# Unit 0's attention output turned on PE, zero matmuls tied to results, and new orders, in a fused window-attention and channel-mix kernel

## Chip, cores and metric

One core of a Trainium2 chip runs the whole program. The metric is the device time of one launch in microseconds (us).

## The reference, cut to what matters

Attention with a causal window of 128 keys and 4 sink keys, followed by a channel mix (a shift by one token, two mixes, and a gated two-layer product). The matmul operands are held in bf16 in the kernel.

```python
# q, k, v: 4 batches, 8 heads, 768 tokens, 64 wide; attention
scores = scale * q @ k.T                       # keep: key < 4, or 0 <= query - key < 128
a = exp(scores - max); a = a / sum(a)
x = (a @ v), heads side by side                # 4 x 768 x 512
# channel mix
x_prev = x shifted by one token
xk = mu_k * x + (1 - mu_k) * x_prev            # and xr with mu_r
k = relu(xk @ w_k)                             # 512 x 1024
out = sigmoid(xr @ w_r) * ((k * k) @ w_v)      # 512 x 512, 1024 x 512
```

## The kernel before

**Units.** The work is cut into 12 units of 256 tokens (u = 0 to 11, three for each batch, T = 0 to 2 within it), each unit into four pairs of heads. A unit goes through four stages: `prepare` (cast q, k, v to bf16; turn q and k by PE transposes or DMA transposes into `qt` and `kt`), `attend`, `mix`, and `ffn`, which follows one unit later.

**Attention.** For a pair, PE writes scores with keys on the partitions and queries in the columns into one of two wide PSUM tiles `sc`. ACT takes the exponential into `e`, DVE multiplies it by the window's mask (L901). PE then multiplies with `e` stationary and the values streaming (L920): the output has queries on the partitions and, per head, 64 columns and one more, the sum of the exponentials, since `vb` carries a column of ones. DVE takes the reciprocal of the four sums (L934, `rec`) and multiplies (L937) into `x`. In units with T > 0 the sink keys come in by a matmul of their own (L858, L873).

**Mix and channel mix.** The mix wants features on the partitions, so `x` is transposed: by PE into a bank (L961) and copied from there by ACT or DVE into `xt` (L970), or, for the units in `XD`, by DMA. DVE subtracts the shifted tile (L997, `td`) and makes `xk` and `xr` (L1010), one step for each 128 features. PE multiplies with `wk_sb` (L1087), ACT takes the relu (L1097, `rl`), DVE squares it (L1109, `kk`), PE multiplies with `wv_h` (L1136), and with `wr_sb` for the gate (L1118), ACT takes the tanh (L1124, `th`), DVE combines (L1145, `ob`), and SP or POOL stores.

**What sets the order.** Every step is an operation of a plan, with a number. The table `ORDER` gives each engine its list of numbers; `CHOICE` gives some steps their engine (ACT, DVE or POOL). `Plan.schedule` walks these lists with costs written into the kernel, and hands out the buffers: four PSUM banks (`bank`), two wide PSUM tiles (`sc`), five tiles `e` and so on. On the chip an engine works its list in order, and a step that waits holds up all behind it. Where the plan sees PE idle before 26 us of its own time, it puts in zero matmuls ("fills", L1160): a tile of zeros times a tile of zeros into a free bank. They wait for no data.

Of the kernel before, what the change touches and what calls it, by code (L numbers as in the profile page):

```python
# [18 lines left out]
    80: "ACT", 81: "POOL", 82: "ACT", 83: "POOL", 84: "POOL", 85: "ACT", 86: "ACT",  # L19
    88: "ACT", 90: "DVE", 96: "POOL", 98: "DVE", 99: "DVE", 101: "DVE", 102: "ACT",  # L20
    103: "ACT", 129: "POOL", 132: "DVE", 135: "POOL", 141: "ACT", 144: "DVE", 151:
    "DVE", 160: "PE/full", 172: "PE/full", 183: "POOL", 186: "DVE", 189: "POOL",
    192: "POOL", 195: "ACT", 196: "DVE", 198: "DVE", 242: "PE/full", 265: "DVE",
    268: "DVE", 271: "POOL", 273: "DVE", 274: "POOL", 277: "DVE", 278: "ACT", 352:
    "POOL", 355: "POOL", 361: "DVE", 380: "DVE", 428: "POOL", 432: "POOL", 438:
    "ACT", 496: "PE/full", 511: "POOL", 516: "ACT", 517: "ACT", 587: "POOL", 591:
    "ACT", 592: "ACT", 628: "POOL", 661: "POOL", 663: "POOL", 665: "ACT", 666:
    "ACT", 675: "DVE", 736: "POOL", 741: "ACT", 785: "POOL", 810: "POOL", 815:
    "DVE", 855: "POOL", 888: "DVE", 889: "ACT", 929: "POOL", 945: "PE/full", 998:
    "DVE", 1002: "DVE", 1006: "DVE", 1010: "DVE", 1019: "POOL",  # L30
# [7 lines left out]
BIAS = ()  # L38

# [55 lines left out]
    ),  # L95
    "DVE": (
# [25 lines left out]
    ),  # L122
    "ACT": (
# [14 lines left out]
    ),  # L138
    "POOL": (
# [3 lines left out]
    ),  # L143
# [8 lines left out]
    ),  # L152
}


class Plan:

    SEM = 40.0
    LAG = {"PE": 163.0, "DVE": 83.0, "ACT": 114.0, "POOL": 60.0, "SP": 90.0}

    def __init__(self):
        self.ops, self.pools, self.buf = [], {}, {}
        self.fill, self.fill_until = None, 0.0  # L170

# [15 lines left out]
    def schedule(self):  # L187
# [43 lines left out]
        while any(lines.values()):  # L231
# [35 lines left out]
            if o["port"]:  # L267
                port[o["engine"]] = t + (0.58 * cost if o["engine"] == "POOL" else cost)
# [953 lines left out]
```

## Time and profile before

| | |
|---|---|
| median of the runs shown | 166.06 us (165.44 the lowest) |
| the profiled execution | 166.53 us |
| its span (first to last instruction) | 164.4 us |
| mean granted clock of TensorE | 0.99 |
| busy: PE, DVE, ACT, POOL | 93%, 91%, 74%, 19% of the span |
| fills: L1165 x8 and L1162 x5, all before 28 us | 5.55 and 1.90 us of PE |

One of the three runs took 530.24 us; the median is the middle of the three. Busy time is the share of the span in which an engine worked on an instruction. PE is the matmul part of TensorE, PEld its weight loads; a chain of waits follows the last instruction back, at each step to what released it.

### The profile page before, as it was taken

The page shows a single profiled execution, that of the slowest core. Times are in us where ns is not written, and L with a number is a line of the kernel's source. Part 1 is how long each engine was busy: PE and PEld are TensorE (multiplying, and loading weights), DVE is VectorE, ACT ScalarE, POOL GpSimd, SP SyncE. Part 2 cuts the span into 40 slices and gives each one's busy share as a digit, 9 for nine tenths or more (in the row PEclk, how much of TensorE's full clock was granted, in tenths as well). Part 3 has the DMA queues.
Part 4 walks back from the last instruction along what each step waited for, and adds up shares of the span by engine and source line. Part 5 has one row for each costly group of instructions (what it writes and reads, how often), then busy time and mean ns, then how long its engine had stood idle before and what let it go on. Part 6 is the DMA issues. An engine that isn't in the chain of part 4 may idle for free.

```text
span 164.4 us, 4647 instructions
## 1 busy us (share of the span) xinstructions
PE 152.6 (93%) x1819; PEld 101.1 (61%) x1838; DVE 149.5 (91%) x383; ACT 121.7 (74%) x198; POOL 31.7 (19%) x61
## 2 busy tenths in 40 slices
PE   7988678899989999999999999999999999999991
PEld 2445557675448658677666766855485756578450
DVE  2599999999999999999999999998899989999931
ACT  3789989999989999999997689782499695152020
POOL 6633341312422023220201001032000100101001
PEclk9999789999999999999999999999999999999999
DMA  5999998999899999889988998999999933251032
GB/s 145 249 357 278 394 333 215 366 394 322 193 271 272 260 219 221 160 176 162 270 216 207 233 232 215 220 219 128 235 165 191 268 94 96 54 205 64 0 144 112
DMA packets 78821, 35.16 MB, mean 214 GB/s; under 512 B 68744, under 2 KB 71056, under 8 KB 78800
## 3 DMA queue, kind: packets, MB, share of 16 engines
q1 hardware_dynamic: 78384, 33.56, 84.0%
q0 software_dynamic: 400, 1.31, 2.3%
q8 instruction: 14, 0.23, 0.6%
q14 instruction: 7, 0.06, 0.1%
q10 hardware_dynamic: 16, 0.00, 0.0%
HBM read 24.12 MB, written 6.29 MB: 185 GB/s over the span
## 4 chain that ended last, share of the span: by engine, by line
PE 62%; DVE 24%; DMA 4%; POOL 4%; issue 3%; ACT 1%; DVEq 0%; POOLq 0%
PE bank L1087 21%; PE bank L1136 18%; PE bank L1118 8%; PE bank L920 6%; DVE e L901 5%; DMA kt<-kb 4%; PE sc L815 4%; DVE xr L1010 3%; DVE xk L1010 3%; DVE x L937 3%; DVE kk L1109 2%; DVE td L997 2%; PE bank L873 1%; POOL hmask L543 1%; PE bank L1057 1%
## 5 line engine op out<-in xcount | busy, mean ns | idle before, releaser
L1087 PE MATMUL bank<-xk,wk_sb 128*128 128x256 bf16 x384 | 47.6, 273 | 1.1 <-ACT rl L1097 0.5
L887 ACT ACTIVATE e<-sc 128x1024 bf16<-128x1024 f32 (+1 forms) x48 | 44.5, 967 | 2.8 <-PE sc L815 2.5
L1136 PE MATMUL bank<-wv_h,kk 128*128 128x512 bf16 x171 | 43.8, 379 | 0.8 <-DVE xk L1010 0.2
L1087 PEld LDWEIGHTS <-wk_sb 128*128 128x128 bf16 x384 | 36.2, 98 | 7.7 <-issue 1.5
L1097 ACT ACTIVATE rl<-bank 128x512 bf16<-128x512 f32 x43 | 25.2, 607 | 8.3 <-PE bank L1087 7.8
L901 DVE TENSOR_TENSOR e<-e,mask 128x1024 bf16<-128x1024 bf16 (+1 forms) x48 | 30.8, 656 | 0.0
L1124 ACT ACTIVATE th<-bank 128x512 f32<-128x512 f32 x24 | 14.3, 612 | 18.2 <-PE bank L1118 11.4
L1136 PEld LDWEIGHTS <-kk 128*128 128x128 bf16 x184 | 17.0, 98 | 16.5 <-issue 0.2
L1010 DVE SCALAR_TENSOR_TENSOR xr<-td,mu_all,xt 128x256 bf16<-128x256 bf16 x48 | 23.8, 507 | 0.0
L1118 PE MATMUL bank<-wr_sb,xr 128*128 128x512 bf16 x90 | 23.3, 379 | 0.3
L1010 DVE SCALAR_TENSOR_TENSOR xk<-td,mu_all,xt 128x256 bf16<-128x256 bf16 x48 | 23.3, 511 | 0.0
L1109 DVE TENSOR_TENSOR kk<-rl 128x512 bf16<-128x512 bf16 x48 | 19.8, 425 | 0.4 <-ACT rl L1097 0.2
L937 DVE TENSOR_TENSOR x<-bank,rec 128x256 bf16<-128x256 f32 x48 | 19.5, 418 | 0.4
L920 PE MATMUL bank<-vb,e 128*128 128x65 bf16 x352 | 16.8, 196 | 1.4 <-DVE e L901 1.1
L1145 DVE SCALAR_TENSOR_TENSOR ob<-th,bank 128x512 f32<-128x512 f32 x23 | 15.6, 681 | 1.9 <-PE bank L1136 1.1
L920 PEld LDWEIGHTS <-e 128*128 128x128 bf16 x352 | 14.2, 99 | 4.5 <-DVE e L901 1.9
L1118 PEld LDWEIGHTS <-xr 128*128 128x128 bf16 x96 | 9.0, 98 | 9.6
L815 PE MATMUL sc<-qt,kt 64*64 64x128 bf16 (+3 forms) x496 | 12.5, 226 | 0.1
L1152 POOL DMA_DIRECT2D out_dram<-ob x5 | 2.8, 570 | 46.8 <-DVE ob L1145 46.8
L815 PEld LDWEIGHTS <-kt 64*64 64x64 bf16 (+1 forms) x496 | 9.0, 106 | 3.3 <-issue 1.0
L997 DVE TENSOR_TENSOR td<-xt 128x512 bf16<-128x512 bf16 x24 | 10.1, 432 | 0.1
L663 POOL CAST kb<-ks 128x512 bf16<-128x512 f32 x6 | 5.3, 884 | 20.4 <-DMA ks<-in_k_dram 17.8
(87 smaller groups left out, 157.2 us busy)
## 6 DMA issues: line engine op xcount, KB each, us to landing
vs<-in_v_dram SPq DMA_DIRECT2D x24, 256.0 KB, 5.3
out_dram<-ob SPq DMA_DIRECT2D x18, 256.0 KB, 3.3
ks<-in_k_dram SPq DMA_DIRECT2D x16, 256.0 KB, 4.2
qs<-in_q_dram SPq DMA_DIRECT2D x12, 256.0 KB, 4.9
qs<-in_q_dram SPq DMA_DIRECT2D x6, 512.0 KB, 7.1
ks<-in_k_dram SPq DMA_DIRECT2D x4, 512.0 KB, 9.3
w<-in_moe_w_k_dram SPq DMA_DIRECT2D x2, 1024.0 KB, 8.6
w<-in_moe_w_v_dram SPq DMA_DIRECT2D x2, 1024.0 KB, 10.6
```

The lines of the kernel that those rows point to most:

```text
L815: nc.tensor.matmul(out=sc[keys, a, o0 + f0 - q0:o0 + f1 - q0], lhsT=lhs[rows, keys], rhs=qs[rows, f0:f1], start=u not in BIAS, stop=True, ...
L887: nc.scalar.activation(out=buf[ek][:, :, lo:], in_=buf[sck][:, :, lo:], func=AF.Exp, scale=scale)
L901: nc.vector.tensor_tensor(out=at, in0=at, in1=m, op=ALU.mult)
L920: nc.tensor.matmul(out=o[:, g, a, :], lhsT=e[:, a, e0:e0 + 128], rhs=rhs, start=(T == 0 and i == 0), stop=(i == len(blocks) - 1), skip_gro ...
L937: P.op("DVE", dve(256), lambda ok=ok, rk=rk, c=c: nc.vector.tensor_tensor(out=buf["x", u][:, :, 128 * c:128 * c + 128].rearrange("p g (a d ...
L1010: nc.vector.scalar_tensor_tensor(out=buf[key][:, c, :], in0=buf[tk][:, i, :], scalar=mu[w][:, c:c + 1], in1=xt[:, c, t0 - 1:t0 + 255], op0 ...
L1087: nc.tensor.matmul(out=ps[:, i, :], lhsT=wk_sb[:, c, 128 * f:128 * f + 128], rhs=xk[:, c, :], start=(c == 0), stop=(c == NC - 1), skip_gro ...
L1097: nc.scalar.activation(out=buf[rk], in_=buf[psk].rearrange("p (i t) -> p i t", i=2), func=AF.Relu)
L1109: P.op("DVE", dve(512, 0.52), lambda f2=f2, rk=rk: nc.vector.tensor_tensor(out=buf["kk", u][:, 2 * f2:2 * f2 + 2, :], in0=buf[rk], in1=buf ...
L1118: nc.tensor.matmul(out=buf[psk], lhsT=buf["xr", u][:, c, 128 * g:128 * g + 128], rhs=wr_sb[:, c, :], start=(c == 0), stop=(c == NC - 1))
L1136: nc.tensor.matmul(out=buf[psk], rhs=wv_h[:, f, :], lhsT=buf["kk", u][:, f, 128 * g:128 * g + 128], start=(f == 0), stop=(f == NF - 1))
L1145: P.op("DVE", dve(512), lambda psk=psk, tk=tk, bk=bk: nc.vector.scalar_tensor_tensor(out=buf[bk], in0=buf[tk], scalar=1.0, in1=buf[psk], o ...
```

## The change

1. **Unit 0 turned** (`TF = (0,)`). For unit 0, PE multiplies with the values stationary and the exponentials streaming. The output has the 64 features of a head on half of the partitions and 256 queries in the columns, so it needs no transpose. The sums come from the same exponentials against a tile of ones, into the other half of the bank: 64 equal rows for each head. DVE takes the reciprocal of all 128x256 sums into `den`, a new pool of two tiles, and multiplies straight into `xt`. For unit 0 the transposes on PE, their copies into `xt` and the products into `x` are gone.
2. **Tied zero matmuls.** After 4.6 us of the plan's time, and up to 28.5, a fill may stream a piece of a tile that DVE or ACT has just made (against the zero weights), and so waits for that result. It may also write into an `sc` tile.
3. **Costs and orders.** Some of the plan's costs are changed, and all of `ORDER` and `CHOICE` is written anew. Over the whole program ACT has 5 instructions fewer, DVE 4, POOL has 7 casts and 8 stores more, and SP 8 stores fewer.

The diff, cut to its core:

```diff
 CHOICE = {
-    80: "ACT", 81: "POOL", 82: "ACT", 83: "POOL", 84: "POOL", 85: "ACT", 86: "ACT",
+    80: "ACT", 81: "POOL", 82: "ACT", 83: "POOL", 84: "POOL", 85: "ACT", 87: "ACT",
...
+TF = (0,)
...
 ORDER = {
     "PE": (
-        91, 94, 107, 100, 97, 78, 118, 110, 115, 105, 130, 136, 143, 133, 139, 126,
+        91, 94, 78, 107, 100, 97, 118, 110, 115, 130, 121, 105, 136, 133, 139, 155,
...
+    PAUSE = 130.0
...
-            if o["engine"] == "PE" and self.fill:
+            if o["engine"] == "PE" and self.fill and before < 4600.0:
...
+            elif o["engine"] == "PE" and self.fill and before < self.fill_until:
+
+                last = max((j for j in o["after"]), key=lambda j: ops[j]["end"], default=None)
+                now, seen = before, before - 500.0
+                while now + 230.0 < t:
...
+                    gates = [j for j, e in done.items() if seen < e + self.SEM <= now and (
+                        last is not None and ops[j]["engine"] == ops[last]["engine"] or
+                        e < t - 700.0)]
+                    gate = max(gates, key=lambda j: done[j], default=None)
...
+                    order.append(("fill", tile_ if name == "bank" else tile_[:, 0, :], 1, gate))
...
+    pool("den", 2, [128, 256], FP32)
...
-                if T > 0:
+                if T > 0 and u not in TF:
...
+            def turned(c=c, ek=ek, ok=ok):
+                e, o = buf[ek], buf[ok]
+                for which in range(2):
+                    c0 = 256 * which
+                    for i in range(4 if T > 0 else 2):
+                        for a in range(2):
+                            h = 2 * c + a
+                            rows = slice(64 * a, 64 * a + 64)
+                            if i == 0:
+                                w, m, q0 = buf["vb", u][:, 0, h, 0:D], e[:, a, 128:384], 0
+                            elif i == 1:
+                                w, m, q0 = buf["vb", u][:, 1, h, 0:D], e[:, a, 384:512], 128
...
+                            if which:
+                                w = ones[:, 0:D] if i < 3 else hmask[:, h, 0:D]
+                            n = m.shape[-1]
+                            nc.tensor.matmul(out=o[rows, c0 + q0:c0 + q0 + n], lhsT=w, rhs=m,
+                                             start=(i == 0), stop=(i == (3 if T > 0 else 1)),
+                                             skip_group_check=True)
+
+            if u in TF:
...
+                P.op("DVE", dve(256), lambda ok=ok, dk=dk: nc.vector.reciprocal(
+                    out=buf[dk], in_=buf[ok][:, 256:512]), r + 1, hold=[ok], reads=[ok],
+                    take=[("den", dk)], writes=[dk])
+                P.op("DVE", dve(256), lambda ok=ok, dk=dk, c=c, xt=xt, t0=t0: nc.vector.tensor_tensor(
+                    out=xt[:, c, t0:t0 + 256], in0=buf[ok][:, 0:256], in1=buf[dk],
+                    op=ALU.mult), r + 1, hold=[ok, dk],
...
+                continue
...
-            if u not in XD:
+            if u in TF:
+                pass
+            elif u not in XD:
...
-    def fill(bank, wide):
-        if wide == 1:
+    def fill(bank, wide, gate=None):
+        if gate is not None:
+            nc.tensor.matmul(out=bank, lhsT=warm[:, 0:128], start=True, stop=True,
+                             rhs=part(gate)().unsqueeze(1).to_broadcast([128, 4, 128]))
+        elif wide == 1:
...
-    P.fill_until = 26000.0
+    P.fill_until = 28500.0
```

**DVE, unit 0's attention to unit 1's first mask.** A number after a name is the tile's. Before, from one of unit 0's last two masks to the first mask of unit 1 (e_97, 1024 columns):

```order
L901 TENSOR_TENSOR e_96<-e_96,mask_147 128x2x384
L970 COPY xt_155<-bank_66 128x2x256
L901 TENSOR_TENSOR e_95<-e_95,mask_147 128x2x384
L659 CAST qb_84<-qs_72 128x2x4x64
L997 TENSOR_TENSOR td_110<-xt_155 128x512
L934 RECIPROCAL rec_103<-bank_66 128x4
L934 RECIPROCAL rec_104<-bank_63 128x4
L937 TENSOR_TENSOR x_107<-bank_66,rec_103 128x2x128
L1010 SCALAR_TENSOR_TENSOR xk_113<-td_110,mu_all,xt_155 128x256
L1010 SCALAR_TENSOR_TENSOR xr_117<-td_110,mu_all,xt_155 128x256
L937 TENSOR_TENSOR x_107<-bank_63,rec_104 128x2x128
L901 TENSOR_TENSOR e_97<-e_97,mask 128x1024
```

And now, up to the same mask (a first wide reciprocal and its product stand just ahead of this piece):

```order
L970 RECIPROCAL den_111<-bank_65 128x256
L973 TENSOR_TENSOR xt_157<-bank_65,den_111 128x256
L970 RECIPROCAL den_110<-bank_64 128x256
L1073 TENSOR_TENSOR td_112<-xt_157 128x512
L934 TENSOR_TENSOR e_96<-e_96,mask_149 128x2x384
L1086 SCALAR_TENSOR_TENSOR xk_115<-td_112,mu_all,xt_157 128x256
L973 TENSOR_TENSOR xt_157<-bank_64,den_110 128x256
L1086 SCALAR_TENSOR_TENSOR xk_115<-td_112,mu_all,xt_157 128x256
L1086 SCALAR_TENSOR_TENSOR xr_119<-td_112,mu_all,xt_157 128x256
L800 TENSOR_TENSOR vsink_155<-bank_66,hmask 128x8x64
L970 RECIPROCAL den_111<-bank_63 128x256
L934 TENSOR_TENSOR e_97<-e_97,mask 128x1024
```

The casts of q and the copy into xt are gone from this piece; four reciprocals of 4 columns have become four of 256, all ahead of e_97's mask.

**PE, ahead of unit 1's first scores** (the matmuls into sc from qt_90 and kt_86). Before:

```order
L920 MATMUL bank_66<-vb_135,e_95 128x65
L1162 LDWEIGHTS warm
L1162 MATMUL bank_65<-warm 128x512
L815 LDWEIGHTS kt_86
L815 MATMUL sc_61<-qt_90,kt_86 64x192
```

Now:

```order
L736 MATMUL bank_63<-ident,qb_83 128x128
L1272 LDWEIGHTS warm
L1272 MATMUL sc_62<-td_112,warm 128x512
L1272 LDWEIGHTS warm
L1272 MATMUL sc_62<-e_96,warm 128x512
L848 LDWEIGHTS kt_86
L848 MATMUL sc_62<-qt_90,kt_86 64x192
```

The fill of zeros alone has become two that read td_112 and e_96, into the tile that the scores write next.

**POOL, in the middle of the program.** Before:

```order
L659 CAST qb_83<-qs_71 128x2x4x64
L757 COPY ksink_152<-kt_88 64x4x4 x2
L659 CAST kb_80<-ks_68 128x2x4x64
L663 CAST kb_81<-ks_69 128x4x128
L740 CAST vb_135<-vs_74 128x8x64
L663 CAST kb_81<-ks_69 128x4x128
```

Now:

```order
L692 CAST qb_83<-qs_71 128x2x4x64
L1228 DMA out_dram<-ob_135 128x512
L692 CAST qb_84<-qs_72 128x2x4x64
L696 CAST kb_81<-ks_69 128x4x128 x2
L773 CAST vb_137<-vs_74 128x8x64
L1228 DMA out_dram<-ob_136 128x512
L773 CAST vb_137<-vs_74 128x8x64
```

Stores of `ob` now stand between the casts for later units.

More of the change, by code (lines that the diff above doesn't have):

```diff
@@ L18 @@
 CHOICE = {
-    80: "ACT", 81: "POOL", 82: "ACT", 83: "POOL", 84: "POOL", 85: "ACT", 86: "ACT",
[L20 to L30, printed above, removed]
+    80: "ACT", 81: "POOL", 82: "ACT", 83: "POOL", 84: "POOL", 85: "ACT", 87: "ACT",
+    88: "ACT", 93: "DVE", 96: "POOL", 98: "DVE", 102: "DVE", 103: "DVE", 129:
+    "POOL", 132: "POOL", 141: "ACT", 179: "POOL", 182: "POOL", 185: "POOL", 188:
+    "POOL", 191: "DVE", 194: "DVE", 201: "DVE", 213: "DVE", 230: "POOL", 250:
+    "PE/full", 264: "POOL", 267: "POOL", 270: "POOL", 274: "DVE", 286: "DVE", 315:
+    "POOL", 348: "POOL", 350: "DVE", 351: "POOL", 397: "POOL", 401: "PE/full", 424:
+    "POOL", 428: "POOL", 430: "POOL", 433: "ACT", 434: "DVE", 509: "POOL", 512:
+    "ACT", 554: "POOL", 581: "POOL", 582: "POOL", 583: "POOL", 585: "POOL", 588:
+    "ACT", 624: "POOL", 659: "POOL", 661: "ACT", 662: "ACT", 700: "POOL", 735:
+    "POOL", 738: "ACT", 781: "POOL", 806: "DVE", 810: "ACT", 811: "ACT", 830: "DVE",
+    847: "POOL", 851: "POOL", 880: "DVE", 885: "ACT", 925: "POOL", 941: "PE/full",
+    970: "DVE", 974: "DVE", 987: "POOL", 991: "POOL", 994: "DVE", 1002: "DVE", 1015:
+    "POOL",
 }
@@ L226, in schedule @@
         slow, gone, fetch = 0.0, 0.0, list(FETCH)
+        done = {}
         released = {key: 0.0 for key in owner}
@@ L254, in schedule @@
             lines[o["engine"]].pop(0)
+            own = []
             for name, key in o["take"]:
@@ L267, in schedule @@
             if o["port"]:
-                port[o["engine"]] = t + (0.58 * cost if o["engine"] == "POOL" else cost)
+                port[o["engine"]] = t + (max(0.58 * cost, cost - 200.0) if o["engine"] == "POOL" else cost)
             end = t + cost + o["lag"]
@@ L297, in schedule @@
             o["start"], o["end"] = t, end
-            if o["engine"] == "PE" and self.fill:
+            if o["engine"] == "PE" and self.fill and before < 4600.0:
                 now = before
-                while t - now > (300.0 if now > 4000.0 else 600.0) and now < self.fill_until:
+                while t - now > (300.0 if now > 4000.0 else 600.0):
                     some = [b for b in free["bank"] if b[0] <= now]
@@ L311, in schedule @@
                     order.append(("fill", self.pools["bank"][b[1]], wide))
+            elif o["engine"] == "PE" and self.fill and before < self.fill_until:
+                last = max((j for j in o["after"]), key=lambda j: ops[j]["end"], default=None)
+                now, seen = before, before - 500.0
+                while now + 230.0 < t:
+                    some = [(b[0], name, b[1], b) for name in ("bank", "sc") for b in free[name]
+                            if b[0] <= now] + [b for b in own if b[1] in ("bank", "sc") and b[0] <= now]
+                    if not some:
+                        now += 60.0
+                        continue
+                    _, name, at_, b = min(some, key=lambda b: b[:3])
+                    tile_ = self.pools[name][at_]
+                    gates = [j for j, e in done.items() if seen < e + self.SEM <= now and (
[3 more added lines that the diff above has]
+                    if gate is not None:
+                        seen = done[gate] + self.SEM
+                    order.append(("fill", tile_ if name == "bank" else tile_[:, 0, :], 1, gate))
+                    now += 225.0
+                    if b is not None:
+                        free[name].remove(b)
+                        free[name].append((now, at_))
+                    now += self.PAUSE if gate is not None else 0.0
+            if o["engine"] in ("DVE", "ACT") and self.gate(i):
+                done[i] = end
             order.append(i)
@@ L630, in cast @@
                    "ACT": (act(1024), emit("ACT"), False)} |
-             ({} if half else {"POOL": (1100.0, emit("POOL"), True)}),
+             ({} if half else {"POOL": (1050.0, emit("POOL"), True)}),
              reads=[(name + "32", i)], writes=writes)
@@ L676, in prepare @@
                            "DVE": (341.0, cast(nc.vector.tensor_copy), True),
-                           "POOL": (620.0, cast(nc.gpsimd.tensor_copy), True)},
+                           "POOL": (600.0, cast(nc.gpsimd.tensor_copy), True)},
                      take=[] if half else [(name + "b", rk)],
@@ L740, in cast @@
                 return lambda: copy(out=buf["vb", u][:, g, :, 0:D], in_=buf["v", u][:, g, :, :])
-            P.op("POOL", 620.0, cast(nc.gpsimd.tensor_copy), rank,
-                 alts={"POOL": (620.0, cast(nc.gpsimd.tensor_copy), True),
+            P.op("POOL", 600.0, cast(nc.gpsimd.tensor_copy), rank,
+                 alts={"POOL": (600.0, cast(nc.gpsimd.tensor_copy), True),
                        "ACT": (515.0, cast(nc.scalar.copy), False),
@@ new lines, in attend @@
+            if u in TF:
+                P.op("PE", 700.0 if T else 360.0, turned, r + 1, mode=5, take=[("bank", ok)],
+                     hold=[ek, ("vb", u)] + ([("vb", u - 1), esk] if T else []), writes=[ok],
+                     reads=[ek, ("vb", u, 0), ("vb", u, 1), "ones0"] +
+                     ([esk, ("vsink", b % 2), "hmask", ("vb", u - 1, 1)] if T else []))
+                xt, t0 = xts[b % 2], 16 + 256 * T
+                dk = ("den", u, k)
+                P.op("DVE", dve(256), lambda ok=ok, dk=dk: nc.vector.reciprocal(
[4 more added lines that the diff above has]
+                    op=ALU.mult), r + 1, hold=[ok, dk],
+                    reads=[ok, dk, "edges"] + ([("xh", u, k - 1)] if k % 2 else []),
+                    writes=[("xt", b % 2, T, k // 2, g) for g in range(2)] if k % 2
+                    else [("xh", u, k)])
+                continue
@@ L975, in mix @@
                      alts={"ACT": (act(512), evacuate(nc.scalar.copy), False),
-                           "DVE": (dve(512, 0.52), evacuate(nc.vector.tensor_copy), True)},
+                           "DVE": (dve(512, 0.52), evacuate(nc.vector.tensor_copy), False)},
                      hold=[psk], reads=[psk],
@@ L1155, in ffn, with part @@
                  alts={"SP": (400.0, store(nc.sync), False),
-                       "POOL": (1100.0, store(nc.gpsimd), True)})
+                       "POOL": (600.0, store(nc.gpsimd), False)})
     zeros = warm.bitcast(FP32)
-    def fill(bank, wide):
-        if wide == 1:
+    def part(i):
+        o = P.ops[i]
+        key = o["writes"][0] if o["writes"] else ()
+        if not isinstance(key, tuple) or len(key) < 2:
+            return None
+        name, u = key[0], key[1]
+        if name == "wk":
+            return lambda: wk_sb[:, 0, 256 * u:256 * u + 128]
+        if name == "wr":
+            return lambda: wr_sb[:, 2 * u, 0:128]
+        if name == "wv":
+            return lambda: wv_h[:, 2 * u, 0:128]
+        if name == "e" and o["engine"] == "DVE":
+            return lambda: buf[key][:, 0, 384:512]
+        if name in ("kb", "qb") and not by_dma(name[0], u):
+            if octet(name[0], u):
+                return lambda: eights(buf[key[:2]])[:, 4 * key[2]].rearrange("p h d -> p (h d)")
+            return lambda: buf[key[:2]][:, 0, 4 * key[2]:4 * key[2] + 2, :].rearrange(
+                "p h d -> p (h d)")
+        if name == "x":
+            return lambda: buf["x", u][:, 0, 128 * key[2]:128 * key[2] + 128]
+        if name == "xt":
+            t0 = 16 + 256 * key[2]
+            return lambda: xts[u][:, 2 * key[3], t0:t0 + 128]
+        if name == "td":
+            return lambda: buf[key][:, 0, 0:128]
+        if name in ("xk", "xr") and len(key) == 3:
+            return lambda: buf[key[:2]][:, key[2], 0:128]
+        if name == "rl":
+            return lambda: buf[key][:, 0, 0:128]
+        if name == "kk":
+            return lambda: buf["kk", u][:, 2 * key[2], 0:128]
+        return None
+    def fill(bank, wide, gate=None):
+        if gate is not None:
+            nc.tensor.matmul(out=bank, lhsT=warm[:, 0:128], start=True, stop=True,
+                             rhs=part(gate)().unsqueeze(1).to_broadcast([128, 4, 128]))
+        elif wide == 1:
             nc.tensor.matmul(out=bank, lhsT=warm[:, 0:128], start=True, stop=True,
@@ L1166, in fill @@
                              rhs=zeros.unsqueeze(1).to_broadcast([128, wide, 128]))
+    P.gate = part
     P.fill = fill
-    P.fill_until = 26000.0
+    P.fill_until = 28500.0
     prepare(0, 0)
```

7 lines of the change are left out of this document (6 added, 1 removed), and 137 rows, old and new, of the table ORDER.

## The prediction

> **What bounds the kernel now.** I read the page's head first, then the busy time by stretch, then the chain of waits, and last the groups by line and shape.
>
> ```profile
> span 164.4 us, 4647 instructions
> PE 152.6 (93%) x1819; PEld 101.1 (61%) x1838; DVE 149.5 (91%) x383; ACT 121.7 (74%) x198; POOL 31.7 (19%) x61
> ...
> core 0: us, PE busy (x) PEld busy (x) DVE busy (x) ACT busy (x) POOL busy (x), PEclk, DMA share, GB/s
> 0.00:9.00 9.00, 7.49 (x36) 3.62 (x37) 4.21 (x20) 5.30 (x8) 5.51 (x22) 1.00 0.82 197
> 9.00:46.00 37.00, 31.39 (x427) 21.54 (x428) 36.59 (x87) 34.00 (x55) 12.80 (x19) 0.95 1.03 321
> 46.00:100.00 54.00, 53.28 (x732) 37.24 (x742) 53.35 (x140) 48.84 (x82) 8.11 (x11) 1.00 1.02 219
> 100.00:140.00 40.00, 39.64 (x495) 25.87 (x499) 37.64 (x100) 28.37 (x47) 3.69 (x7) 1.00 0.88 183
> 140.00:161.00 21.00, 20.77 (x136) 12.79 (x134) 17.27 (x42) 5.16 (x9) 1.42 (x3) 1.00 0.27 91
> ```
>
> The first line of each stretch's numbers is its length, then the busy time of PE, weight loads, DVE, ACT and POOL. From 9 to 46 us DVE is busy 36.59 of 37.00 us while PE leaves 5.6 us empty and runs at 0.95 of its clock: DVE sets that stage. From 46 us PE is full (53.28 of 54.00), but DVE is just as full (53.35); only after 100 us does DVE have air, 2.4 us up to 140. The chain of waits, in order of time, says the same:
>
> ```profile
> 8.95 0.68 DVE qt L726
> 9.63 0.94 DVE e L901 x2
> ...
> 44.69 0.75 DVE kk L1109
> 45.44 0.61 DVE ob L1145
> 46.09 0.38 PE bank L703 x4
> 46.47 0.86 PE bank L1136 x4
> ```
>
> Up to 46 us its links are nearly all DVE's, from there nearly all PE's. So a microsecond more of DVE work before 46 us goes to PE late by the same microsecond; with both engines full behind it, hardly anything makes it up. The turned unit 0 puts its new work just there, between 9 and 20 us.
>
> **The change, part by part.** First the DVE. The rows that price it:
>
> ```profile
> L934 DVE RECIPROCAL rec<-bank 128x4 f32<-128x4 f32 x48 | 7.5, 172 | 1.4 <-PE bank L920 1.0
> L609 DVE COPY mu_all<-bank 128x8 f32<-128x8 f32 x1 | 0.2, 155 | 0.0
> L937 DVE TENSOR_TENSOR x<-bank,rec 128x256 bf16<-128x256 f32 x48 | 19.5, 418 | 0.4
> L1145 DVE SCALAR_TENSOR_TENSOR ob<-th,bank 128x512 f32<-128x512 f32 x23 | 15.6, 681 | 1.9 <-PE bank L1136 1.1 <-issue 0.5 <-ACT th L1124 0.2
> L970 DVE COPY xt<-bank 128x512 bf16<-128x512 bf16 x5 | 2.0, 410 | 0.0
> L726 DVE COPY qt<-bank 128x512 bf16<-128x512 bf16 x1 | 0.7, 681 | 0.0
> L659 DVE CAST qb<-qs 128x512 bf16<-128x512 f32 x3 | 1.7, 555 | 0.0
> L659 DVE CAST kb<-ks 128x512 bf16<-128x512 f32 x1 | 0.8, 839 | 0.0
> L668 DVE CAST kb<-ks 128x512 bf16<-128x512 f32 x1 | 0.5, 508 | 2.0 <-DMA ks<-in_k_dram 2.0
> L740 DVE CAST vb<-vs 128x512 bf16<-128x512 f32 x4 | 1.7, 420 | 0.0
> L1101 DVE TENSOR_SCALAR rl<-bank 128x512 bf16<-128x512 f32 x5 | 3.3, 686 | 0.3 <-PE bank L1087 0.3
> ```
>
> What leaves DVE: four small reciprocals (4 x 0.172 = 0.69), two copies into xt (0.82), one of qt (0.68), three casts of q (1.67) and two of k (0.84 + 0.51): 5.2 us. The four products into x become four into xt with the same 256 columns out of a bank, 0.418 each both times: nothing. What comes besides the reciprocals: two casts of k in another layout and one of v, priced by the v cast (3 x 0.420 = 1.26), and one relu (0.69): 1.95 us.
>
> The term that decides is the four new reciprocals, 128x256 where there were 128x4. No row has one. Ordinary work out of a bank costs (681 - 418) / 256 = 1.03 ns per column. At that rate the copy of 8 columns, 155 ns, leaves 147 ns fixed. The reciprocal of 4 columns takes 172 ns, 25 ns over that fixed part, where 4 ordinary columns would take 4. Read as throughput, 25 / 4 = 6.25 ns a column, and 256 columns take 147 + 1600 = 1.75 us. Read as a longer way through the unit that overlaps with the next column, a column costs 1.03 ns and the whole 0.42 us, as the product does. These are my bounds: 0.42 us below; above, by the slowest of them:
>
> ```profile
> L934 DVE RECIPROCAL rec<-bank x48: 144/174/184, 10.5 to 140.1; 128x4 f32<-128x4 f32 x48
> ```
>
> 184 ns gives (184 - 147) / 4 = 9.25 ns a column, 2.5 us each. The shortest, 144 ns, lies under the fixed part and speaks for the lower bound. I take 1.75 us: the mean and the median agree on it, and of the two readings it is the one that needs no second effect. Four are 7.0 us. [...]
>
> So DVE's line grows by 7.0 + 1.95 - 5.2 = 3.7 us. Where it sits, the order of DVE shown with the change tells: all four reciprocals stand ahead of unit 1's first mask (e_97), in one queue with td, xk and xr, which feed the first products of the channel mix. In the traced execution that stretch ran from the first mask to the start of e_97's:
>
> ```profile
> 9.55 1.02 DVE L901 TENSOR_TENSOR e<-e,mask 128x768 bf16<-128x768 bf16 x2
> ...
> 17.23 1.12 DVE L901 TENSOR_TENSOR e<-e,mask 128x1024 bf16<-128x1024 bf16 x1
> ```
>
> Those 7.7 us lose four small reciprocals, one product, two casts and a copy (0.69 + 0.42 + 1.11 + 0.41) and gain 7.0 for the wide reciprocals, a cast and a mix (0.42 + 0.51): 5.3 us more, so the mask of e_97 starts near 22.5 us. Later stretches give 1.6 of it back.
>
> **POOL and DVE.** Seven more casts go to POOL (26 become 33). What a POOL cast does to DVE's work beside it, the mixes show:
>
> ```profile
> L1010 DVE SCALAR_TENSOR_TENSOR xk<-td,mu_all,xt x48: 454/477/1160, 15.8 to 147.1; 128x256 bf16<-128x256 bf16 x48
> L1010 DVE SCALAR_TENSOR_TENSOR xr<-td,mu_all,xt x48: 456/477/1250, 16.5 to 152.9; 128x256 bf16<-128x256 bf16 x48
> ...
> L1010 DVE SCALAR_TENSOR_TENSOR xr<-td,mu_all,xt 128x256 bf16<-128x256 bf16 x48 | 23.8, 507 | 0.0
> ...
> 21.06 1.04 POOL L626 CAST wk_sb<-w 128x1024 bf16<-128x1024 f32 x1 [2.23 <-DMA w<-in_moe_w_k_dram]
> 21.13 1.25 DVE L1010 SCALAR_TENSOR_TENSOR xr<-td,mu_all,xt 128x256 bf16<-128x256 bf16 x1
> ```
>
> Some of the 96 mixes are stretched, the worst to 1.25 us beside a POOL cast; mean less median is 0.03 us, so 2.9 us over all 96, about 0.11 us for each of the 26 casts. Seven more: 0.8 us, with 0 below and 7 x 0.77 = 5.4 us above. Together DVE carries 4.5 us more.
>
> **PE, ACT and the gated zero matmuls.** PE loses 24 of the 65-column products and 8 transposes, and gains 32 turned matmuls, whose two head halves write different column halves.
>
> ```profile
> 15.56 0.29 PE L784 MATMUL bank<-qt,ksink 128*32 128x256 bf16 x4
> 19.13 1.09 PE L920 MATMUL bank<-vb,e 128*128 128x65 bf16 x16
> ...
> 69.98 0.59 PE bank L920 x16
> 29.21 0.39 PE L703 MATMUL bank<-ident,qb 128*128 128x128 bf16 x4
> 81.45 1.75 PE bank L1087 x16
> ```
>
> Sixteen wk matmuls of 256 columns take 1.75 us, 0.11 each; four column quarters of 256 take 0.29 together, so column parts do run side by side. A turned pair is then between 0.33 us (halves together, 768 columns) and 0.66 (one after the other): 1.3 to 2.6 us for four, against 0.8 for the transposes that go (0.39 for four) and 0.9 to 1.6 for the products (0.59 or 1.09 for sixteen). PE changes by -1.1 to +0.9 us, and I take 0: the 5.6 us that PE stands empty before 46 us cover either, and without that cover the dearer end would cost 0.9. ACT loses about five steps of 0.6 us; at 34.0 of 37.0 us it is not the limit there, so nothing. The zero matmuls are now tied to results and some stand ahead of real work: in the order of PE shown with the change, two that read td_112 and e_96 stand ahead of unit 1's first scores, where one that waits for no data stood. td_112 and e_96's mask come behind the first three wide reciprocals; unit 1's scores, their exponentials on ACT and the sink scores queue behind that. Unit 1's masks stand behind the fourth reciprocal on DVE anyway, so I give the tie 0 to 1.75 us (one reciprocal's delay, once more) and take 0. The clock that the fills can win back, 5% of 37 us or 1.9 us of PE time, falls where DVE is the limit: 0.
>
> **Sum.** DVE is later by 4.5 us at the end of its stage. Of that the 2.4 us of air after 100 us can absorb part; PE hardly waits there, so I take a quarter, 0.6. The profiled execution took 166.53 us, span and surroundings: 166.53 + 3.9 = 170.4. It lies 0.47 over the median of 166.06, so the forecast is **170.0 us**, 2.4% slower. Two per cent, 3.3 us, is about what a measurement of this kernel can tell from no change.
>
> **Rivals.** *The wide reciprocal runs at one column per 1.03 ns.* For it speaks the 144 ns minimum; against it the 25 ns for 4 columns in the mean. DVE then grows by 4 x 0.42 + 1.95 - 5.2 + 0.8 = -0.8 us: 166.06 - 0.8 = 165.3, not slower. If POOL's casts cost nothing and unit 0's shorter way lets PE fill 2 us of its 5.6 empty ones too, 162.5. It decides below (5.2 - 1.95 - 0.8) / 4 = 0.61 us a reciprocal, where DVE's line no longer grows. *The wide reciprocal costs 8 ns a column*, midway between median and slowest, (6.75 + 9.25) / 2: 147 + 2048 = 2.2 us each, 1.8 more in all, 171.8. [...] *The ties and the stores become the wait.* Stores move from SP to POOL, 5 to 13, and casts for later units now stand behind them in POOL's queue, as its order shown with the change has it:
>
> ```profile
> POOL out_dram L1152 <- DVE ob L1145: 46.8, 5, 15.7
> ```
>
> Five stores already hold POOL for 46.8 us, harmlessly, since few casts stand behind. If eight more hold casts, and DVE's lag makes each later, PE loses another 1 to 3 us: 172.
>
> **Chances.** Forecast 0.52 (168.3 to 171.5, the spread of POOL's and the absorbed terms), of which 0.36 lies over 169.4. Ordinary-rate reciprocal 0.27, of which 0.07 below 162.7. Eight nanoseconds 0.13, ties and stores 0.08. Slower: 0.36 + 0.13 + 0.08 = 0.57; same: 0.16 + 0.20 = 0.36; faster 0.07. The range 164.6 to 172.8 takes in the middle of the rival on the other side and both slow ones; a fifth lies outside.
>
> **What would show it.** A group of four reciprocals 128x256 near 1.75 us each, unit 1's first 1024-column mask starting near 22.5 us instead of 17.2, the chain on DVE well past 46 us, and PE's empty time from 9 to 46 us grown by about 4 us show it right. Reciprocals near 0.42 us make it wrong at the first step. Reciprocals near 1.75 us with a time below 168 make the step from DVE's line to the end wrong.

## The result, and the profile after

The changed kernel takes 171.63 us (median of 4 runs, 170.93 to 171.84) against 166.12 us in the runs beside it: a ratio of 1.0297, 95% interval 1.0242 to 1.0353. It is slower by 3.0%; the forecast was 170.0 us, 2.4% slower, with a range to 172.8.

The profiled execution took 171.68 us. The head of its page, and its busy time by stretch (the columns are those of before: length, then busy time of PE, weight loads, DVE, ACT and POOL, then the granted clock):

```profile
span 170.0 us, 4712 instructions
PE 158.2 (93%) x1863; PEld 102.2 (60%) x1863; DVE 155.0 (91%) x379; ACT 119.7 (70%) x193; POOL 39.4 (23%) x76
...
9.00:46.00 37.00, 31.06 (x416) 20.66 (x414) 36.54 (x75) 28.75 (x45) 14.05 (x23) 0.91 1.03 317
46.00:100.00 54.00, 53.06 (x693) 35.17 (x694) 53.00 (x134) 46.56 (x78) 11.95 (x18) 1.00 0.92 196
100.00:140.00 40.00, 39.91 (x500) 26.60 (x497) 38.58 (x100) 30.72 (x52) 4.57 (x8) 1.00 1.08 197
```

The span grew by 170.0 - 164.4 = 5.6 us and DVE's busy time by 155.0 - 149.5 = 5.5 us. DVE is as full as it was in its stage (36.54 of 37.00), while ACT there fell from 34.00 to 28.75 us, PE's clock from 0.95 to 0.91, and DVE got through 75 instructions where it had done 87.

The new operation itself, by source line and then by group, and the start of e_97's mask in the timeline:

```profile
L970 DVE RECIPROCAL den<-bank x4: 1742/1753/1758, 10.8 to 20.7; 128x256 f32<-128x256 f32 x4
...
L970 DVE RECIPROCAL den<-bank 128x256 f32<-128x256 f32 x4 | 7.0, 1752 | 0.2 <-PE bank L959 0.2
...
20.65 1.76 DVE L970 RECIPROCAL den<-bank 128x256 f32<-128x256 f32 x1 [0.15 <-PE bank L959]
22.33 0.63 DVE L934 TENSOR_TENSOR e<-e,mask 128x1024 bf16<-128x1024 bf16 x1
```

Each of the four took 1.75 us (minimum, median and maximum agree to 1%), 7.0 us in all, and unit 1's first mask of 1024 columns starts at 22.33 us instead of 17.23. The chain of waits of the changed kernel, its shares and then pieces in order of time:

```profile
PE 52%; DVE 31%; DMA 6%; issue 4%; SPq 3%; ACT 2%; POOL 0%; DVEq 0%
...
10.84 1.76 DVE den L970
...
13.47 1.68 DVE den L970
...
15.59 1.66 DVE den L970
...
139.66 1.21 DVE e L934 x2
```

And, for comparison, the shares and one late piece of the kernel before, then the shares of the changed kernel with copies in place of the four reciprocals (the first experiment below):

```profile
PE 62%; DVE 24%; DMA 4%; POOL 4%; issue 3%; ACT 1%; DVEq 0%; POOLq 0%
...
79.39 0.76 DVE xk L1010
```

```profile
PE 54%; DVE 32%; issue 4%; DMA 3%; ACT 3%; SPq 2%; DVEq 0%
```

Three of the four reciprocals are links of it. DVE's links come back as late as 141 us, but links of DVE past 46 us are no mark of the reciprocals: the kernel before has some from 77 to 80 us, and with copies DVE has 32% of the chain in this trace and 24% in another.

### The profile page after: what moved, and what is told of

Read it like the earlier page. It is cut to its first block, busy times and chain, and to the rows that moved or that the text cites. A ratio compares the mean times of both kernels' runs of the same rounds, so it can differ in the third digit from the quotient of the medians.

```text
span 170.0 us, 4712 instructions
## 1 busy us (share of the span) xinstructions
PE 158.2 (93%) x1863; PEld 102.2 (60%) x1863; DVE 155.0 (91%) x379; ACT 119.7 (70%) x193; POOL 39.4 (23%) x76
## 4 chain that ended last, share of the span: by engine, by line
PE 52%; DVE 31%; DMA 6%; issue 4%; SPq 3%; ACT 2%; POOL 0%; DVEq 0%
PE bank L1212 17%; PE bank L1163 15%; PE bank L1194 7%; DVE e L934 6%; DVE xr L1086 4%; PE bank L994 4%; DVE xk L1086 3%; DMA out_dram<-ob 3%; DVE x L1011 3%; DVE den L970 3%; DMA ks<-in_k_dram 3%; PE sc L848 3%; DVE ob L1221 2%; DVE kk L1185 2%; DVE td L1073 2%
## 5 line engine op out<-in xcount | busy, mean ns | idle before, releaser
L920 ACT ACTIVATE e<-sc 128x1024 bf16<-128x1024 f32 (+1 forms) x48 | 43.8, 956 | 4.8 <-PE sc L848 4.6
L1212 PE MATMUL bank<-wv_h,kk 128*128 128x512 bf16 x184 | 45.0, 379 | 0.5 <-DVE wv_h L657 0.5
L934 DVE TENSOR_TENSOR e<-e,mask 128x1024 bf16<-128x1024 bf16 (+1 forms) x48 | 31.7, 672 | 0.1
L1086 DVE SCALAR_TENSOR_TENSOR xr<-td,mu_all,xt 128x256 bf16<-128x256 bf16 x48 | 24.8, 531 | 0.0
L1011 DVE TENSOR_TENSOR x<-bank,rec 128x256 bf16<-128x256 f32 x44 | 17.7, 414 | 0.2
L1228 POOL DMA_DIRECT2D out_dram<-ob x13 | 7.1, 551 | 46.5 <-DVE ob L1221 41.4
L994 PE MATMUL bank<-vb,e 128*128 128x65 bf16 x328 | 15.8, 194 | 1.4 <-DVE e L934 1.1
L994 PEld LDWEIGHTS <-e 128*128 128x128 bf16 x328 | 13.3, 97 | 4.9 <-DVE e L934 1.5
L848 PE MATMUL sc<-qt,kt 64*64 64x128 bf16 (+4 forms) x496 | 13.1, 232 | 0.0
L773 POOL CAST vb<-vs 128x512 bf16<-128x512 f32 x9 | 6.8, 758 | 20.1 <-DMA vs<-in_v_dram 17.7
```

The source lines that it names most:

```text
L848: nc.tensor.matmul(out=sc[keys, a, o0 + f0 - q0:o0 + f1 - q0], lhsT=lhs[rows, keys], rhs=qs[rows, f0:f1], start=u not in BIAS, stop=True, ...
L920: nc.scalar.activation(out=buf[ek][:, :, lo:], in_=buf[sck][:, :, lo:], func=AF.Exp, scale=scale)
L934: nc.vector.tensor_tensor(out=at, in0=at, in1=m, op=ALU.mult)
L994: nc.tensor.matmul(out=o[:, g, a, :], lhsT=e[:, a, e0:e0 + 128], rhs=rhs, start=(T == 0 and i == 0), stop=(i == len(blocks) - 1), skip_gro ...
L1011: P.op("DVE", dve(256), lambda ok=ok, rk=rk, c=c: nc.vector.tensor_tensor(out=buf["x", u][:, :, 128 * c:128 * c + 128].rearrange("p g (a d ...
L1086: nc.vector.scalar_tensor_tensor(out=buf[key][:, c, :], in0=buf[tk][:, i, :], scalar=mu[w][:, c:c + 1], in1=xt[:, c, t0 - 1:t0 + 255], op0 ...
```

## Experiments

### What the wide reciprocals cost: copies in their place

One word changes: the four wide reciprocals become copies of the same columns. Order, buffers, waits and tied fills stay.

```diff
-                nc.vector.reciprocal(out=buf[dk], in_=buf[ok][:, 256:512])
+                nc.vector.tensor_copy(out=buf[dk], in_=buf[ok][:, 256:512])
```

> The changed kernel with its four wide reciprocals replaced by copies of the same 128x256 out of the bank (the division in unit 0 is left out). Theory A, the reciprocals' length alone: each goes from 1.75 to about 0.42 us, DVE's line loses 4 x 1.34 = 5.3 us, and with both engines full behind it nearly all of that reaches the end: 171.6 - 5.3 = 166.3, between 165.5 and 167.2, equal to the kernel before. Rival B, the ties, the stores and the new orders carry a good part: no lower than 168.5.

Measured: 167.5 us, ratio 1.0049 (1.0011 to 1.0087), 0.3 us above the range of theory A and well below rival B. The same kernel once more, in a later set of runs:

> The copies alone once more, on the same chip as the two with the stores on SP, for a paired comparison (unit 0's division is left out): 167.0 to 168.0 us by both theories.

Measured: 166.94 us, ratio 1.0024 (0.9983 to 1.0064). So of the 3.0% loss 2.5 to 2.7 points, 4.1 to 4.5 us, go with the reciprocals, which are 4 x (1.752 - 0.418) = 5.3 us longer than products of that size. Two more pairs of kernels further down differ in this one word alone: without ties 1.0359 and 1.0047, 3.1 points or 5.2 us, and with the stores on SP 1.0268 and 0.9971, 3.0 points or 4.9 us. So by these ratios 4.1 to 5.2 of the 5.3 us arrive; their intervals allow one to two microseconds either way. How the delay travels is best seen in one line for each kernel, all masks by source line (duration in ns, then start of the first and of the last in us). Before, then copies in the later set (with its page head and e_97's mask), then changed, and last the page head, e_97's mask and all masks of the copies in the first set:

```profile
L901 DVE TENSOR_TENSOR e<-e,mask x48: 525/680/1122, 9.5 to 138.2; 128x1024 bf16<-128x1024 bf16 x32, 128x768 bf16<-128x768 bf16 x16
```

```profile
PE 154.3 (94%) x1842; PEld 100.6 (61%) x1863; DVE 150.6 (92%) x379; ACT 119.5 (73%) x193; POOL 41.1 (25%) x76
...
16.76 0.68 DVE L934 TENSOR_TENSOR e<-e,mask 128x1024 bf16<-128x1024 bf16 x1
...
L934 DVE TENSOR_TENSOR e<-e,mask x48: 520/679/958, 9.0 to 138.6; 128x1024 bf16<-128x1024 bf16 x32, 128x768 bf16<-128x768 bf16 x16
```

```profile
L934 DVE TENSOR_TENSOR e<-e,mask x48: 521/680/1190, 9.3 to 144.1; 128x1024 bf16<-128x1024 bf16 x32, 128x768 bf16<-128x768 bf16 x16
```

```profile
PE 156.6 (94%) x1863; PEld 101.2 (61%) x1863; DVE 152.0 (91%) x379; ACT 119.6 (72%) x193; POOL 41.8 (25%) x76
...
17.36 0.68 DVE L934 TENSOR_TENSOR e<-e,mask 128x1024 bf16<-128x1024 bf16 x1
...
L934 DVE TENSOR_TENSOR e<-e,mask x48: 522/680/1112, 9.3 to 140.5; 128x1024 bf16<-128x1024 bf16 x32, 128x768 bf16<-128x768 bf16 x16
```

With copies in the later set, e_97's mask starts at 16.76 us and the last mask at 138.6; with reciprocals at 22.33 and 144.1: 5.6 us later at the first and 5.5 at the last. In this pair of traces, what DVE loses by 22 us is still missing, whole, at 144, and the spans, 164.5 and 170.0 us, differ by the same 5.5. But that trace is of the fastest of its kernel's executions, 166.24 us. Against the trace of the first set, an execution of 168.13 us with a span of 166.4, the first of these masks is 5.0 us later and the last 3.6. One pair of traces can't tell to a microsecond how much arrives; the three pairs of ratios, from several executions each, do it better.

### The same delay once more, and the same delay in the old order

Each wide reciprocal twice in the changed kernel; and, in the kernel before, four wide reciprocals whose result nobody reads, each just behind one of unit 0's small ones.

```diff
 # twice, in the changed kernel
-                nc.vector.reciprocal(out=buf[dk], in_=buf[ok][:, 256:512])
+                [nc.vector.reciprocal(out=buf[dk], in_=buf[ok][:, 256:512]) for _ in range(2)]
 # in the kernel before, unit 0 only
+                nc.vector.reciprocal(out=wide, in_=buf[ok][:, 0:256])
```

> The changed kernel with each wide reciprocal done twice into the same tile (no output changes). Theory A: DVE's line grows by 4 x 1.67 = 6.7 us (1.75 less the 0.08 by which neighbours overlap) and the end moves by nearly all of it: 177.3 to 178.5. Rival B, the delay is absorbed behind the stage by DVE's later air: under 176.

> The kernel before with one wide reciprocal (128x256 out of the same bank, into a tile that nobody reads) behind each of unit 0's four small ones; orders, ties and stores as before. Theory A, a microsecond on DVE before 46 us is a microsecond at the end whatever the order: 4 x 1.67 = 6.7 us, ratio 1.038 to 1.042. Rival B, the old order has slack that the new one lost: ratio 1.02 to 1.03.

Twice: 178.45 us, ratio 1.0749 (1.0679 to 1.0819). In the old order: 171.84 us, ratio 1.0314 (1.0252 to 1.0376). First the rows of the kernel with each reciprocal twice (page head, group, stretch, masks), then those of the old order:

```profile
PE 159.4 (90%) x1863; PEld 103.0 (58%) x1863; DVE 161.2 (91%) x383; ACT 119.5 (68%) x193; POOL 39.6 (22%) x76
...
L970 DVE RECIPROCAL den<-bank 128x256 f32<-128x256 f32 x8 | 14.0, 1753 | 0.2
...
9.00:46.00 37.00, 25.75 (x347) 17.46 (x346) 36.21 (x63) 22.43 (x35) 11.44 (x18) 0.82 0.84 269
...
L934 DVE TENSOR_TENSOR e<-e,mask x48: 522/682/1092, 9.6 to 150.7; 128x1024 bf16<-128x1024 bf16 x32, 128x768 bf16<-128x768 bf16 x16
```

```profile
L936 DVE RECIPROCAL wide<-bank 128x256 f32<-128x256 f32 x4 | 6.9, 1734 | 0.0
...
9.00:46.00 37.00, 29.46 (x403) 21.69 (x402) 36.10 (x80) 28.94 (x47) 11.35 (x17) 0.77 1.02 308
...
L902 DVE TENSOR_TENSOR e<-e,mask x48: 524/680/1257, 9.8 to 143.9; 128x1024 bf16<-128x1024 bf16 x32, 128x768 bf16<-128x768 bf16 x16
```

The second 7.0 us move the last mask by another 6.6 (144.1 to 150.7): nearly all of it arrives. In the old order 6.9 us move it by 5.7 (138.2 to 143.9), and the time by 3.1%, 5.2 us: about three quarters arrive and the rest finds cover. That lies between what the two theories expected. The loss needs neither the turned matmuls nor the new order; the reciprocals alone make it in the kernel before.

### What a column of the reciprocal costs

The four calls get 32, 64, 128 and 256 columns; where columns remain they are copied, so that part of unit 0's division is left out.

```diff
-                nc.vector.reciprocal(out=buf[dk], in_=buf[ok][:, 256:512])
+                nc.vector.reciprocal(out=buf[dk][:, 0:32 << k], in_=buf[ok][:, 256:256 + (32 << k)])
+                # the other columns, where k < 3: tensor_copy
```

> The changed kernel; the four reciprocals of unit 0 take 32, 64, 128 and 256 columns, and a copy fills the rest of the tile (the division is left out there). Theory A, 6.25 ns a column over 147 ns fixed: 0.35, 0.55, 0.95 and 1.75 us. Rival, a step or another rate at small widths: any of the first three off that line by more than 0.05 us.

Measured: 170.22 us, one run. Its groups:

```profile
L970 DVE RECIPROCAL den<-bank 128x256 f32<-128x256 f32 x1 | 1.7, 1742 | 0.0
L970 DVE RECIPROCAL den<-bank 128x128 f32<-128x128 f32 x1 | 0.9, 948 | 0.0
L970 DVE RECIPROCAL den<-bank 128x64 f32<-128x64 f32 x1 | 0.5, 542 | 0.0
L970 DVE RECIPROCAL den<-bank 128x32 f32<-128x32 f32 x1 | 0.4, 358 | 0.1
```

From 32 to 256 columns: (1742 - 358) / 224 = 6.18 ns a column, over 160 ns fixed; 64 and 128 columns lie on that line to within 15 ns. So the cost grows with every column, which the reading as a longer way that overlaps does not give.

### The tied fills

The fills read the zero tile again, in the changed kernel and in the kernel with copies.

```diff
-        if gate is not None:
-            nc.tensor.matmul(out=bank, lhsT=warm[:, 0:128], start=True, stop=True,
-                             rhs=part(gate)().unsqueeze(1).to_broadcast([128, 4, 128]))
-        elif wide == 1:
+        if wide == 1:
```

> The changed kernel with every tied zero matmul reading the zero tile instead of a result: the same number of fills at the same places, none waits for data. Theory A: DVE sets the stage and the scores behind the ties are not needed earlier, 171.6 within 0.5. Rival B: the ties hold PE up to one reciprocal's length, 169.9 to 170.5.

> Both edits: copies instead of the wide reciprocals (unit 0's division is left out) and untied fills. Theory A: as with the copies alone, within 0.5 us, since with short reciprocals the tied results come on time. Rival B: a further 0.5 to 1.5 us below the copies alone, when the ties cost by themselves.

Measured: 172.95 us, ratio 1.0359 (1.027 to 1.0449), for the changed kernel without ties; 1.0047 (1.0009 to 1.0085) for the copies without ties, against 1.0049 with them. The first lies above the 171.1 to 172.1 us expected, and away from the rival that the ties hold PE, but its interval and that of the changed kernel overlap. The ties cost nothing that these runs can tell, though in the changed kernel the fill that reads td_112 does hold PE:

```profile
17.59 0.59 PE L1272 MATMUL sc<-td,warm 128*128 128x512 bf16 x1 [0.57 <-DVE td L1073]
```

PE stood 0.57 us for it, ahead of unit 1's scores. The masks of unit 1 stand behind the fourth reciprocal in any case, so that wait is covered, as was taken.

### POOL's casts

Seven casts whose result nobody reads, and one memset of their source, set among POOL's early ones in the kernel before; and, in the kernel with copies, four of the early casts given to ACT.

```diff
 # kernel before: after seven of POOL's early casts
+                nc.gpsimd.tensor_copy(out=dump, in_=src32)     # 128x512
 # kernel with copies: CHOICE, four casts (vb 1, qb 2 twice, qb 3)
-    182: "POOL", 188: "POOL", 264: "POOL",
+    142: "ACT", 182: "ACT", 188: "ACT", 264: "ACT",
 # and the four numbers moved from POOL's list in ORDER to ACT's
```

> The kernel before with seven more casts of 128x512 on POOL, into a tile that nobody reads, each behind one of its early casts (and one memset of their source). Theory C: DVE's masks and mixes are stretched by some 0.5 us a cast, DVE's busy time grows by 3 to 4 us and the ratio is 1.015 to 1.025. Rival D: 0.8 us on DVE, ratio 1.002 to 1.007. POOL's own casts come later by 0.6 to 0.9 us each, which both leave out.

> The changed kernel with copies for the wide reciprocals (unit 0's division is left out), and four of POOL's early casts (one of v for unit 1, two of q for unit 2, one of q for unit 3) moved to ACT. Theory C, POOL's casts stretch DVE's work beside them by some 0.5 us each: DVE's busy time falls by 1.5 to 2.5 us against the copies alone and the ratio from 1.005 to 0.990 to 0.998. Rival D, POOL's casts cost DVE little, 0.1 each as I priced them: busy time falls by under 0.7 us and the ratio stays at 1.003 or rises with ACT's added 2.5 us.

Casts added to the kernel before: 168.65 us, ratio 1.0147 (1.0088 to 1.0207). Casts given to ACT: 168.5 us, ratio 1.0145 (1.0089 to 1.0201). Head, stretch and the added group of the first; head and one group of the second:

```profile
PE 154.2 (93%) x1838; PEld 101.7 (61%) x1838; DVE 150.5 (90%) x383; ACT 121.5 (73%) x198; POOL 41.3 (25%) x69
...
9.00:46.00 37.00, 31.00 (x421) 21.70 (x420) 35.48 (x85) 32.23 (x52) 20.53 (x26) 0.91 1.03 319
...
L534 POOL CAST dump<-src 128x512 bf16<-128x512 f32 x7 | 5.8, 822 | 0.1
```

```profile
PE 158.8 (95%) x1877; PEld 102.5 (61%) x1877; DVE 150.4 (90%) x379; ACT 121.7 (73%) x197; POOL 39.3 (24%) x72
...
L926 DVE TENSOR_TENSOR e<-e,mask 128x1024 bf16<-128x1024 bf16 x32 | 21.3, 682 | 0.8 <-ACT e L912 0.7
```

With seven more casts DVE's work is longer by 1.0 us (149.5 to 150.5), 0.15 us each, but the time by 2.4. DVE's idle time in its stage, 37.00 - 35.48 = 1.5 us where it was 0.4, says that about half of this is not stretched work but work that comes late. POOL was busy 9.6 us longer (31.7 to 41.3), 5.8 of it in the seven casts; which of its late casts DVE missed was not tried apart. Theory C had the ratio roughly right and DVE's 3 to 4 us wrong, rival D the other way round. Four casts less on POOL did not help: ACT carries 2.1 us more than in the copies (119.6 to 121.7), masks now wait for its exponentials, and the kernel is 1% worse than the copies. DVE's busy time of 150.4 cannot be set against the copies: they had 152.0 in one trace and 150.6 in the other. So DVE's busy time differs by more than a microsecond between executions of one kernel, and both experiments leave the size of the stretch open: the 1.0 us of the first lies inside that difference too.

### The stores on POOL

The eight earliest stores that the change put on POOL go back to SP, in the kernel with copies and in the changed one.

```diff
-    230: "POOL", 315: "POOL", 397: "POOL", 554: "POOL", 624: "POOL", 700: "POOL", 781: "POOL", 851: "POOL",
+    230: "SP", 315: "SP", 397: "SP", 554: "SP", 624: "SP", 700: "SP", 781: "SP", 851: "SP",
```

> Unit 0's division is left out (the four wide reciprocals are copies of the same 128x256 columns), and the eight earliest of the stores of out that the change put on POOL go back to SP. The pair with copies alone ran 167.5 us, 0.5% over the kernel before, though DVE's own list is shorter by the prediction's figures. Theory D (stores on POOL hold the casts behind them, which come late to PE): 0.5 to 1.5 us better than the copies alone, to 166.0 to 167.0 us. Rival (the 0.5% lies in the order and in DVE's stretch beside POOL's casts): within 0.5 us of the copies alone, POOL's idle time aside.

> The changed kernel whole, with its wide reciprocals, and the same eight stores on SP. Theory D: the lag of DVE makes each store later and so each cast behind it; 1 to 3 us better than 171.6, to 168.6 to 170.6 us. Rival (the reciprocals alone carry the loss): 171.0 to 172.2 us.

Copies with stores on SP: 165.99 us, ratio 0.9971 (0.993 to 1.0011), against 166.94 and 1.0024 for the copies on the same chip: 0.95 us better, the size expected of theory D, though the two intervals overlap. Changed kernel with stores on SP: 171.54 us, ratio 1.0268 (1.0207 to 1.0328): not told apart from 1.0297. The stores are not where the 3% went. What waits POOL has, in the copies of the later set and then in the copies with stores on SP (us in total, times, longest):

```profile
POOL out_dram L1228 <- DVE ob L1221: 39.3, 8, 10.2
...
POOL vb L773 <- DMA vs<-in_v_dram: 18.8, 3, 16.2
```

```profile
POOL out_dram L1219 <- DVE ob L1212: 25.8, 4, 13.6
...
POOL vb L764 <- ACT rl L1164: 22.6, 1, 22.6
...
POOL vb L764 <- DMA vs<-in_v_dram: 13.5, 3, 12.2
```

A store that waits for DVE is replaced, in good part, by a cast that waits for its tile or its data.

The first of these also hints at the limit of what can be had. With the division at the price of a copy, and without the stores on POOL, the turned unit 0 ends at 0.997 of the kernel before, with 1 inside the interval. A wide division on DVE that cost no more than a copy was not seen, so a version built from these parts is not likely to beat the kernel before by a measurable amount; none was run, nor a division elsewhere or on fewer columns.

## Why the prediction was right, step by step

**What bounds the kernel: right.** A DVE delay before 46 us came out at the end for the most part: 4.1 to 5.2 us of the 5.3 between copies and reciprocals, and at the last mask 6.6 of 7.0 for the second set of reciprocals and 5.7 of 6.9 in the old order. The sign named for it, a chain on DVE well past 46 us, was seen but tells nothing, since the kernel before and the copies have such links too.

**The wide reciprocal: right, and to the hundredth of a microsecond by luck.** 1.75 us was taken from 25 ns for 4 columns; 1.752 was measured, and 6.18 ns a column from 32 to 256 columns against 6.25. This is what decided. That the cost is paid per column was right. The size hung on a difference in which one nanosecond is worth 64 ns at 256 columns, and two errors met in it: the line through the four widths has 160 ns fixed, not 147, and would give the small reciprocal 185 ns, not 172. With 160 the same row would have said 3 ns a column and 0.93 us. The first rival, 1.03 ns a column and 165.3 us, fell at the price. But copies have that price, and they gave ratios of 1.0024 and 1.0049, not 165.3 / 166.06 = 0.995: the rest of that sum was too kind by 0.7 to 0.9 points, 1.2 to 1.6 us. The second rival, 8 ns a column, gave 171.8, close to the time measured and for the wrong reason: the reciprocal did not cost it.

**DVE's line: short by one term.** Forecast +4.5 us, measured +5.5. The instructions themselves (7.0 + 1.95 - 5.2 = 3.7) leave 1.8 us for the stretch of DVE's other work, where 0.8 was taken inside bounds of 0 to 5.4. This is one trace of each kernel, and the two traces of the copies differ by 1.4, so neither the size nor POOL as its cause is shown. The means of DVE's other work went up in part; these are mixes and masks of the changed kernel, where before had 507 for `xr`, 511 for `xk` and 572 for the narrow masks:

```profile
L1086 DVE SCALAR_TENSOR_TENSOR xr<-td,mu_all,xt 128x256 bf16<-128x256 bf16 x48 | 24.8, 531 | 0.0
L1086 DVE SCALAR_TENSOR_TENSOR xk<-td,mu_all,xt 128x256 bf16<-128x256 bf16 x48 | 23.0, 504 | 0.1
L934 DVE TENSOR_TENSOR e<-e,mask 128x768 bf16<-128x768 bf16 x16 | 9.5, 598 | 0.0
```

Mean less median of mixes, from which the 0.8 came, does not see what the masks lose. In the copies, where DVE's own list is 1.6 us shorter than before (4 x 0.418 + 1.95 - 5.2) and its busy time 1.1 to 2.5 longer, the stretch is 2.7 to 4.1 us. Why it is larger there than with wide reciprocals is open.

**What the air after 100 us absorbs: taken 0.6, not settled.** DVE filled that air in part (2.4 us empty before, 40.00 - 38.58 = 1.4 now). Against the copies' faster trace the last mask is as late as the first of unit 1, against the other 1.4 us less; by the three pairs of ratios 0.1 to 1.2 of 5.3 us are absorbed somewhere. On paper the two terms (1.0 and 0.6) make up the 1.6 us between 170.0 and 171.6, but how these divide is not shown. The 171.63 us measured lie just over the 168.3 to 171.5 that the forecast kept for itself, and inside the whole range.

**e_97's mask: right.** 22.5 us was forecast, 22.33 measured.

**PE, ACT and the ties: nothing found against 0.** The turned matmuls overlap in part, between the two bounds:

```profile
10.28 0.36 PE L959 MATMUL bank<-e,vb 128*64 128x256 bf16 x4
10.47 0.33 PE L959 MATMUL bank<-e,ones 128*64 128x256 bf16 x4
10.76 0.36 PE L959 MATMUL bank<-e,vb 128*64 128x256 bf16 x4
```

A pair's eight start 0.48 us after the eight before (10.28 to 10.76), where 0.33 stood for halves side by side and 0.66 for one after the other. Four pairs take 1.9 us, against 0.8 for the transposes and 0.9 to 1.6 for the products that went: -0.5 to +0.2 us.

**The clock: no gain in time, as taken.** With copies PE ran at 1.00 of its clock from 9 to 46 us (before 0.95), and the kernel was no faster; no run left the fills out, so whether they win back any clock is not shown. Nor does the clock explain the loss: the changed kernel with its fills untied had 0.95 there, as before, and lost no less.

```profile
9.00:46.00 37.00, 30.18 (x417) 20.30 (x416) 36.71 (x75) 28.99 (x45) 14.56 (x23) 0.95 1.04 315
```

**PE's empty time from 9 to 46 us: the wrong sign to look for.** It was to grow by 4 us; it is 37.00 - 31.06 = 5.9 after 5.6. Fills count as busy, and matmuls took longer where the granted clock was lower: in the changed kernel the transposes of `qb` took 311 ns each from 16 to 22 us, at 0.50, and 218 ns from 30 to 46 us, at 1.00. Against the copies, which have the same list for PE, it did grow, by 2.8 us:

```profile
9.00:46.00 37.00, 33.90 (x464) 22.67 (x466) 36.84 (x86) 33.17 (x52) 15.93 (x23) 1.00 1.06 325
```

464 matmuls done there against 416 say more than the empty time does.

**Ties and stores as the wait, 172 us: fell.** Fills without ties, and in another run stores on SP, leave the changed kernel where it is as far as the intervals tell.

## What to carry to other kernels

An operation whose cost is wanted at 256 columns may stand in the trace at 4: what it takes over the fixed cost there, divided by the columns, is a first price (here 25 / 4 = 6.25 ns a column), and it is worth taking that as throughput until a run says otherwise. That it came out to 1% here (6.18 measured) was luck, since an error of a few nanoseconds at 4 columns is multiplied by 64; a run at two or three widths is the sound way. Here DVE filled a stage (36.59 of 37.00 us), PE and DVE were full behind it (53.28 and 53.35 of 54.00), and most of a delay at its start arrived at the end, 4.1 to 5.2 of 5.3 us; so broadcasting a sum over 64 rows to save transposes was paid at the price of the division, 6.18 ns a column. To see such a delay travel, compare the start of the same instruction, early and late in the two programs, rather than the busy or empty time of the engine that suffers, and do it with more than one trace of each.

## What the runs showed of the hardware

The reciprocal on DVE costs 6.18 ns a column out of a bank for 32 to 256 columns over 160 ns fixed, six times the 1.03 ns that (681 - 418) / 256 gives for other work out of a bank, and its four calls in the changed kernel, with POOL busy for 14.05 of the 37.00 us of DVE's stage, lay between 1742 and 1758 ns. DVE's busy time is not a property of the program alone: two traces of the same kernel with copies have 152.0 and 150.6 us of it. Seven casts of 0.82 us more on POOL, with one memset, cost the kernel before 2.4 us, though DVE's work grew by only 1.0.
